# An attention and gated feed-forward kernel on one core: the copies that make high parts go from VectorE to ScalarE, the splits of x are spread out, and SyncE's transfers follow the program

## The chip, the core and the metric

The kernel runs on one core of a Trainium2 chip. The metric is device time in microseconds (us). The core has a matrix engine (TensorE, "PE" in the profile; its weight loads are "PEld"), VectorE ("DVE"), ScalarE ("ACT"), GpSimd ("POOL") and SyncE ("SP"). Here SP issues every transfer of the program and computes nothing. Each engine runs its own list of instructions in order; an instruction whose input is not ready holds up everything behind it on that engine.

## What is computed

```python
def _attn_ref(q, k, v, f):                      # q, k, v: (8, 8, 576, 64), f: (8, 8, 576)
    scores = matmul(q, k.T) / sqrt(64)
    cum = cumsum(log(clip(f, 1e-4, 1)))
    scores = where(causal, -1e9, scores + cum[:, None] - cum[None, :])
    attn = exp(scores - max(scores)); attn = attn / (sum(attn) + 1e-9)
    return matmul(attn, v)
def _moe_ref(x, w_in, w_out):                   # x: (4608, 512), from attention's output
    h = x @ w_in                                # (4608, 2048)
    g = h * erf(softplus(h))
    return g @ w_out                            # (4608, 512)
```

Everything is float32 at the interface; the weights arrive as 64-bit floats and are turned into 32-bit ones on the chip.

## The kernel before

**Attention** takes the 64 pairs of batch and head two at a time: 32 pairs p, each in two halves, so 64 steps t in a software pipeline of six stages (lines 648 to 698). In step t the program has: loads of q, k and the decay c for the pair after next and of v for the pair before (`load`, line 472; `load_values`, line 485), scores on PE, exps on ACT, the reduction on DVE, the normalization and the masks on POOL, transposes and values on PE, and the store of a finished pair to a scratch tensor `xt_d` in DRAM (line 611). q, k and c have three buffers each, v has two. Between these stand pieces of work that turn the first weights into pairs of parts (`weight_work`, line 332).

**The feed-forward part** wants near-float32 products from float32r matmuls. So every operand is kept as two parts: a high part, which is the value rounded to float32r by a copy, and a low part, which is the value minus the high part. Each product is then three matmuls. For x the work is a two-by-two block scheme with seven products instead of eight: seven combinations of four loaded blocks of x (`t[0]` to `t[3]`, and the sum `t[4]`) are split into parts, in seven slots `x_0` to `x_6`, and multiplied with seven combinations of w_in.

The work is cut into 12 visits v (six blocks of 768 tokens, once for each half of the 2048 columns) of four steps each; step n is step k = n mod 4 of visit n div 4. A step (`step`, line 241) goes through seven products i = 0 to 6. For each it has six matmuls `m<-x,wi` (`product`, line 131), then the work that takes the result out of PSUM (`consume`, line 155: ACT for i = 0 and 2, as tiles `sa` and `h`; DVE for the others, as `sb`, `sc` and `h`), then about five of the 36 matmuls `y<-wo,gh` and `y<-wo,gl` (`down`, line 192) of step n - 2. PSUM has two banks for m: a product can only begin when the earlier result in its bank was taken out.

In step n the gates of step n - 1 are made: four softplus and four erf on ACT (lines 175 and 178; each of the two functions needs a table load), and in `gate` (line 180), after product 1, for each of four tiles on DVE `e = e * h` (line 184) and the high part `gh` (line 188), and on POOL the low part `gl` (line 189).

In the last step of a visit (k = 3) x of the next visit is split (`split_x`, line 111): after products 0 to 4 one slot each, in the order `x_0`, `x_5`, `x_1`, `x_4`, `x_6`, and after products 0 and 1 of the next step `x_2` and `x_3`. The high parts are DVE's (line 121) but for `x_4` and `x_6`, which are ACT's (line 119); the low parts are POOL's but for `x_0` and `x_6`, which are DVE's (line 123). Two differences that use other slots' sources are DVE's: line 125 right behind `x_0`, and `last_sum` (line 129) behind product 3, ahead of the instruction that takes out product 4. It overwrites `t[1]`, which POOL reads for the low part of `x_1`. The loads of `t` for a visit stand at the start of step k = 2 of the visit before (`load_x`, line 96).

From step 2 to step 18 a filler list of 108 items (`FILL`, line 63) is worked off between the products: it loads a piece of the weights (`lraw`), then ACT takes a magnitude (line 356; often with a table load ahead of it and another behind it), DVE does four operations on the bits, and each finished 32-bit block is split by a copy (line 383, DVE) and a difference (line 384, POOL). A piece has one buffer for `lraw`: the next load is issued when `join` (line 371) has been done (line 373), and the next magnitude is the next item on the list. Some parts go to DRAM and are loaded again for the second half of the columns.

**What sets the order.** The kernel marks ACT, PE, DVE and POOL as ordered by the program's own order (`ORDERED`, line 20). SP is not in that set: its transfers are put in order by a scheduler, which may move a transfer ahead of others that the program has first.

Of the kernel before, what the change touches and what calls it, by code (L numbers as in the profile page):

```python
# [19 lines left out]
ORDERED = {mybir.EngineType.Activation, mybir.EngineType.PE, mybir.EngineType.DVE, mybir.EngineType.Pool}  # L20
# [52 lines left out]
class Moe:  # L73

    def __init__(self, tc, xt_d, part_d, out, xs):
# [6 lines left out]
        self.fill, self.reload = [], None  # L82
# [28 lines left out]
    def split_x(self, v, i):  # L111

        nc = self.nc
        t, r = self.t[v], XSLOT[i]
        src = t[{0: 0, 5: 0, 1: 1, 4: 4, 6: 2, 2: 1, 3: 3}[r]]
        x = self.x_tile(v, r)
        h, l = x[:, 0], x[:, 1]
        if i in (3, 4):
            nc.scalar.copy(out=h, in_=src)
        else:  # L120
            nc.vector.tensor_copy(out=h, in_=src)  # L121
        eng = nc.vector if i in (0, 4) else nc.gpsimd
        eng.tensor_tensor(out=l, in0=src, in1=h.bitcast(F32), op=ALU.subtract)  # L123
        if i == 0:
            nc.vector.tensor_tensor(out=t[0], in0=t[4], in1=t[0], op=ALU.subtract)

    def last_sum(self, v):
        t = self.t[v]
        self.nc.vector.tensor_tensor(out=t[1], in0=t[1], in1=t[0], op=ALU.subtract)
# [50 lines left out]
    def gate(self, n, q):  # L180

        nc = self.nc
        e, h = self.e.pop((n, q)), self.h.pop((n, q))
        nc.vector.tensor_mul(e, e, h)  # L184
# [3 lines left out]
        nc.vector.tensor_copy(out=gh, in_=e)  # L188
# [52 lines left out]
    def step(self, n):  # L241
# [13 lines left out]
        for i in range(7):  # L255
# [8 lines left out]
            if after and k == HU - 1 and i < 2:  # L264
                self.split_x(v + 1, i)
# [25 lines left out]
def attention_moe(ctx, tc, q2, k2, vp, f, w_in, w_out, out):  # L291
# [40 lines left out]
    def weight_work(pieces, buf):  # L332
# [42 lines left out]
        def parts(m, to, dst, src, cut=None):  # L375
# [7 lines left out]
            nc.vector.tensor_copy(out=vh, in_=src)  # L383
# [40 lines left out]
    def early_buf(kind, m, shape, dt=F32):  # L424
        slot = {"raw": m % 2, "top": 2 + m % 2, "tt": 4}[kind]
# [6 lines left out]
    load_weight, todo = weight_work([(a, i) for a in range(HU) for i in range(2)] + [(0, 2), (0, 3)], early_buf)  # L432
# [325 lines left out]
```

## Time and profile before

| | |
|---|---|
| time of the runs, us | 1264.35, 1259.42, 1255.23; median 1259.42 |
| the profiled execution, us | 1255.74, its span 1254.0 |
| mean granted clock of PE | 0.963 |
| attention, to the first product of step 0 | 0 to 331.57 |
| steps 0 and 1, beside the end of attention | 331.57 to 362.14 |
| steps 2 to 19, with the weights' pieces up to step 18 | 362.14 to 755.19 |
| steps 20 to 46 | 755.19 to 1216.65 |
| the last step, and the matmuls `y` of the last two | 1216.65 to 1254.0 |
| busy share of the span | PE 90%, DVE 72%, ACT 54%, POOL 54% |

A row of the profile's groups has the line, the engine, the operation and the tiles (written <- read, buffer numbers left out), the shapes and the count; then busy time in us and the mean ns of one; then the idle time of the engine just ahead of these instructions, and what ended most of it. A row of a timeline has the start in us, the duration, engine, line and tiles, and in brackets the idle time ahead of it with what ended it. A row of windows has a stretch of the span, its length, the busy us (and count) of PE, PEld, DVE, ACT and POOL in it, the granted clock of PE, the share of the transfer engines and GB/s.

### The profile page before, as it was taken

To read this page: it belongs to the slowest core of one execution; us is meant where nothing else is said; L and a number is where in the kernel's file an instruction comes from. 1 tells how busy PE (TensorE), PEld (TensorE's weight loads), DVE (VectorE), ACT (ScalarE), POOL (GpSimd) and SP (SyncE) were. 2 spreads that over 40 slices of the span, in tenths; PEclk is the share of its full clock that TensorE was granted. 3 is DMA by queue.
4 is the path that set the end of the run, shared out by engine and by line. 5 is a ranking of instruction groups with operands and counts; after the bars stand their busy time and mean duration, and the time that the engine had idled before them with its cause. 6 is when DMAs were issued, how large, how long until landed. Compare 5 with 4: busy or idle time off the path is not lost. (4 is left out here: it accounts for less than half of the span.)

```text
span 1254.0 us, 21300 instructions
## 1 busy us (share of the span) xinstructions
PE 1124.1 (90%) x7384; PEld 969.9 (77%) x7384; DVE 906.4 (72%) x1990; ACT 674.4 (54%) x1452; POOL 679.0 (54%) x808
## 2 busy tenths in 40 slices
PE   8988899999997687887786889989898989899898
PEld 7877788887885576776675778878787878788787
DVE  5886799998768568688767786656667666766565
ACT  4876688888653454465354654544344434445442
POOL 4785778888935327355445464444545353544422
PEclk8999999999998888998998899999999999999999
DMA  7666877876221231443322413443131312122032
GB/s 262 195 215 193 282 242 244 250 225 194 68 87 48 86 109 51 125 137 93 109 92 72 157 50 132 179 179 115 51 101 38 113 38 78 37 67 84 1 101 68
DMA packets 74908, 155.83 MB, mean 124 GB/s; under 512 B 7472, under 2 KB 27184, under 8 KB 73776
## 3 DMA queue, kind: packets, MB, share of 16 engines
q1 hardware_dynamic: 74800, 154.47, 38.0%
q8 instruction: 59, 0.97, 0.3%
q14 instruction: 49, 0.40, 0.1%
HBM read 114.44 MB, written 39.99 MB: 123 GB/s over the span
## 5 line engine op out<-in xcount | busy, mean ns | idle before, releaser
L147 PE MATMUL m<-x,wi 128*128 128x384 f32 x2016 | 429.2, 349 | 87.0 <-DVE sc L168 47.2
L147 PEld LDWEIGHTS m<-x,wi 128*128 128x128 f32 x2016 | 372.1, 194 | 133.7 <-DVE sc L168 60.2
L206 PE MATMUL y<-wo,gh 128*128 128x512 f32 x1152 | 385.5, 403 | 18.6 <-DVE wo L383 16.4
L189 POOL TENSOR_TENSOR gl<-e,gh 128x384 fp32r<-128x384 f32 x192 | 228.1, 1188 | 296.5 <-DVE gh L188 270.5
L206 PEld LDWEIGHTS y<-wo,gh 128*128 128x128 f32 x1152 | 220.4, 193 | 53.8 <-DVE wo L383 17.7
L206 PE MATMUL y<-wo,gl 128*128 128x512 f32 x576 | 231.7, 402 | 0.0
L557 POOL TENSOR_SCALAR pr<-pr,st 128x576 f32<-128x576 f32 (+4 forms) x320 | 167.9, 545 | 58.6 <-DVE st L553 30.2
L175 ACT ACTIVATE e<-h 128x384 f32<-128x384 f32 x192 | 93.6, 521 | 194.5 <-DVE h L171 194.1
L188 DVE CAST gh<-e 128x384 fp32r<-128x384 f32 x192 | 186.1, 969 | 6.6
L547 ACT ACTIVATE pr<-pr,st 128x576 f32<-128x576 f32 (+3 forms) x320 | 176.6, 557 | 8.0 <-DVE st L535 8.0
L535 DVE CUSTOM_DVE_ANT_0 pr<-s,c 128x576 f32<-128x576 f32 (+3 forms) x320 | 136.8, 487 | 36.5 <-PE s L519 25.8
L123 POOL TENSOR_TENSOR x<-t,x 128x768 fp32r<-128x768 f32 x55 | 105.0, 1916 | 92.4 <-DVE x L121 85.7
L206 PEld LDWEIGHTS y<-wo,gl 128*128 128x128 f32 x576 | 111.5, 194 | 17.9
L184 DVE TENSOR_TENSOR e<-e,h 128x384 f32<-128x384 f32 x192 | 106.2, 553 | 22.0 <-ACT e L178 21.9
L596 PE MATMUL o<-pt,v 128*64 128x128 f32 (+1 forms) x1920 | 106.0, 264 | 11.0 <-DMA v<-in_vp_dram 7.6
L596 PEld LDWEIGHTS o<-pt,v 128*64 128x64 f32 x1920 | 97.2, 140 | 21.1 <-DVE st L535 5.1
L515 PE MATMUL s<-k,q 64*128 64x320 f32 (+4 forms) x768 | 109.8, 411 | 2.1 <-DVE st L535 2.1
L578 ACT COPY pt<-t 128x512 f32<-128x512 f32 x128 | 73.9, 577 | 69.9 <-PE t L569 68.1
L569 PE MATMUL t<-ident,pr 128*128 128x128 f32 x800 | 105.1, 277 | 4.7 <-ACT pt L578 2.7
L569 PEld LDWEIGHTS t<-ident,pr 128*128 128x128 f32 x800 | 87.3, 140 | 17.6 <-issue 11.1
L171 DVE TENSOR_TENSOR h<-m,sb 128x384 f32<-128x384 f32 x96 | 53.0, 554 | 60.8 <-PE m L147 59.9
L515 PEld LDWEIGHTS s<-k,q 64*128 64x128 f32 x768 | 72.6, 189 | 30.5 <-issue 15.3
(96 smaller groups left out, 1147.4 us busy)
## 6 DMA issues: line engine op xcount, KB each, us to landing
v<-in_vp_dram SPq DMA_DIRECT2D x32, 576.0 KB, 6.5
c<-cum_d SPq DMA_DIRECT2D x62, 288.0 KB, 5.6
t<-xt_d SPq DMA_DIRECT2D x44, 384.0 KB, 3.3
q<-in_q_dram SPq DMA_DIRECT2D x32, 320.0 KB, 3.2
k<-in_k_dram SPq DMA_DIRECT2D x32, 288.0 KB, 4.3
xt_d<-xo SPq DMA_DIRECT2D x32, 288.0 KB, 5.7
part_d<-yo SPq DMA_DIRECT2D x36, 256.0 KB, 2.0
yo<-part_d SPq DMA_DIRECT2D x36, 256.0 KB, 2.9
```

What stands on the lines that cost most here:

```text
L123: eng.tensor_tensor(out=l, in0=src, in1=h.bitcast(F32), op=ALU.subtract)
L147: nc.tensor.matmul(out=ps, lhsT=w[:, wp, ws], rhs=x[:, xp, kd], start=first and kd == 0 and j == 0, stop=kd == 1 and j == 2 and i in (1, 2 ...
L184: nc.vector.tensor_mul(e, e, h)
L188: nc.vector.tensor_copy(out=gh, in_=e)
L189: nc.gpsimd.tensor_tensor(out=gl, in0=e, in1=gh.bitcast(F32), op=ALU.subtract)
L206: yield nc.tensor.matmul(out=y[tb], lhsT=g[:, cs], rhs=w[:, f, wp], start=first, stop=last)
L515: nc.tensor.matmul(out=s[j][:, at:at + k1 - k0], lhsT=q[h, PAD + START[i]:PAD + END[i]], rhs=k[h, k0:k1], start=i > 0, stop=i not in (0, 3))
L535: nc.vector.tensor_tensor_reduce(out=to[:, ::-1] if j else to, in0=score, in1=decay_, scale=-0.125, scalar=BIG, op0=ALU.add, op1=ALU.min, ...
L547: nc.scalar.activation(out=seg, in_=seg, func=AF.Exp, bias=st[:, 0, j, m:m + 1], scale=-1.0, accum_out=st[:, 1, j, m:m + 1])
L557: nc.gpsimd.tensor_scalar(out=seg, in0=seg, scalar1=st[:, 2, j, m:m + 1], scalar2=1.0, op0=ALU.mult, op1=ALU.mult)
L569: nc.tensor.transpose(out=b[:, n * P:(n + 1) * P], in_=probs[t][:, at:at + P], identity=ident)
L596: nc.tensor.matmul(out=o[h, to:to + width], lhsT=v[:, ch, h], rhs=pt[:, at[j]:at[j] + width], start=n == 0, stop=n == len(parts) - 1, skip ...
```

## The change

SP joins the ordered engines. `gate` is cut in two: the products `e * h` stay after product 1, and a new `halve` after product 2 makes `gh` by ACT and `gl` by POOL. All high parts of x are now ACT's, in every visit; the low parts of slots 0 and 5 are DVE's, the other five POOL's. In the last step of a visit the splits stand behind products 2 to 6 and ahead of the next step's first product. The high parts of the later weights' pieces (those of steps 2 to 18) are ACT's. During attention the splits of the first visit begin at step 44 of 64 with the loads, go on with one piece of work each at steps 46, 48, 50 and 52, and end with one slot each in steps 59 to 63; before, all of it stood in steps 56 to 63. The early weights' buffers move from slots 0 to 4 to slots 1 to 4 and 6. No instruction is added or dropped; five high parts of x per visit, four `gh` per step and the high parts of the later weights go from DVE to ACT.

```diff
-ORDERED = {mybir.EngineType.Activation, mybir.EngineType.PE, mybir.EngineType.DVE, mybir.EngineType.Pool}
+ORDERED = {mybir.EngineType.Activation, mybir.EngineType.PE, mybir.EngineType.DVE, mybir.EngineType.Pool,
+           mybir.EngineType.SP}
...
-    def split_x(self, v, i):
...
-        if i in (3, 4):
-            nc.scalar.copy(out=h, in_=src)
-        else:
-            nc.vector.tensor_copy(out=h, in_=src)
-        eng = nc.vector if i in (0, 4) else nc.gpsimd
-        eng.tensor_tensor(out=l, in0=src, in1=h.bitcast(F32), op=ALU.subtract)
-        if i == 0:
-            nc.vector.tensor_tensor(out=t[0], in0=t[4], in1=t[0], op=ALU.subtract)
...
+    def split_x(self, v, r):
+
+        t = self.t[v]
         x = self.x_tile(v, r)
+        self.src[r] = t[{0: 0, 5: 0, 1: 1, 4: 4, 6: 2, 2: 1, 3: 3}[r]]
+        self.nc.scalar.copy(out=x[:, 0], in_=self.src[r])
+
+    def rest_x(self, v, r):
+
+        x = self.x[v, r]
+        eng = self.nc.vector if r in (0, 5) else self.nc.gpsimd
+        eng.tensor_tensor(out=x[:, 1], in0=self.src[r], in1=x[:, 0].bitcast(F32), op=ALU.subtract)
+
+    def both_x(self, v, r):
+        self.split_x(v, r)
+        self.rest_x(v, r)
+
+    def late_sum(self, v, j):
         t = self.t[v]
-        self.nc.vector.tensor_tensor(out=t[1], in0=t[1], in1=t[0], op=ALU.subtract)
+        self.nc.vector.tensor_tensor(out=t[j], in0=t[4 if j == 0 else 1], in1=t[0], op=ALU.subtract)
...
     def gate(self, n, q):
+        self.nc.vector.tensor_mul(self.e[n, q], self.e[n, q], self.h.pop((n, q)))
+
+    def halve(self, n, q):
...
-        nc.vector.tensor_copy(out=gh, in_=e)
+        nc.scalar.copy(out=gh, in_=e)
         nc.gpsimd.tensor_tensor(out=gl, in0=e, in1=gh.bitcast(F32), op=ALU.subtract)
...
+        if up and v and k == 0:
+            self.both_x(v, 3)
         if gates:
             self.softplus(n - 1, 0)
...
-            if after and k == HU - 1 and i < 2:
-                self.split_x(v + 1, i)
...
-            if after and k == HU - 1 and 2 <= i < 5:
+            if after and k == HU - 1 and i == 2:
+                self.split_x(v + 1, 0)
+            if gates and i == 2:
+                for q in range(4):
+                    self.halve(n - 1, q)
+            if after and k == HU - 1:
                 if i == 3:
-                    self.last_sum(v + 1)
-                self.split_x(v + 1, i)
-            if up and v and k == 0 and i < 2:
-                self.split_x(v, 5 + i)
+                    self.rest_x(v + 1, 0)
+                    self.late_sum(v + 1, 0)
+                    self.both_x(v + 1, 1)
+                elif i == 4:
+                    self.both_x(v + 1, 5)
+                elif i == 5:
+                    self.late_sum(v + 1, 1)
+                    self.both_x(v + 1, 4)
+                elif i == 6:
+                    self.both_x(v + 1, 6)
+                    self.both_x(v + 1, 2)
...
-            nc.vector.tensor_copy(out=vh, in_=src)
+            cast(out=vh, in_=src)
...
-            if NH - 8 <= t < NH:
-                start_x(t - NH + 8)
+            if NH - 20 <= t < NH - 10 and t % 2 == 0:
+                start_x((t - NH + 20) // 2)
+            if NH - 5 <= t < NH:
+                start_x(t - NH + 10)
...
-                                        + [(a, i) for a in range(HU, NU) for i in range(4)], late_buf)
+                                        + [(a, i) for a in range(HU, NU) for i in range(4)], late_buf, nc.scalar.copy)
```

In the listings that follow, a row is one instruction in its engine's list: line, operation, tile written <- tiles read, size. The line numbers of the changed kernel are some 16 to 23 higher.

**SP, in the middle of attention.** `ta` and `tb` are the four blocks of x for the first visit, loaded from `xt_d`; `xt_d<-xo` is the store of a finished pair, which they read. Before:

```order
L476 DMA q_937<-in_q_dram 128x640
L477 DMA k_938<-in_k_dram 128x576
L482 DMA c_941<-cum_d 128x576 x2
L488 DMA v_944<-in_vp_dram 128x1152
L611 DMA xt_d<-xo_868 128x576
L443 DMA ta<-xt_d 128x384
L346 DMA raw_1678<-in_w_in_dram 128x2x512
L476 DMA q_1105<-in_q_dram 128x640
L477 DMA k_1106<-in_k_dram 128x576
L482 DMA c_1109<-cum_d 128x576 x2
L488 DMA v_1112<-in_vp_dram 128x1152
```

After, the same two pairs, and then the place where the loads of x now stand:

```order
L497 DMA q_937<-in_q_dram 128x640
L498 DMA k_938<-in_k_dram 128x576
L503 DMA c_941<-cum_d 128x576 x2
L509 DMA v_944<-in_vp_dram 128x1152
L632 DMA xt_d<-xo_868 128x576
L362 DMA raw_1021<-in_w_in_dram 128x2x512
L497 DMA q_1105<-in_q_dram 128x640
L498 DMA k_1106<-in_k_dram 128x576
L503 DMA c_1109<-cum_d 128x576 x2
L509 DMA v_1112<-in_vp_dram 128x1152
```

```order
L632 DMA xt_d<-xo_3658 128x576
L460 DMA ta<-xt_d 128x384 x4
L460 DMA tb<-xt_d 128x384 x4
L362 DMA raw_3898<-in_w_out_dram 128x1024
L497 DMA q_3900<-in_q_dram 128x640
```

Before, the scheduler had put each of the eight loads of x right behind a store to `xt_d`, ahead of the next pair's q, k, c and v, in the first third of attention; now all eight stand together at step 44.

**DVE, in the last step of a visit without weights' work** (`sc` takes out product 3, the tiles `h_3`, `h_1`, `h_2` products 4, 5 and 6). Before, from the last gate on:

```order
L184 TENSOR_TENSOR e_3_10904<-e_3_10904,h_3_10852 128x384
L188 CAST gh_3_10946<-e_3_10904 128x384
L121 CAST x_1_10964<-t_1_10747 128x768
L168 TENSOR_TENSOR sc_10979<-m_2_10972,sb_10925 128x384
L129 TENSOR_TENSOR t_1_10747<-t_1_10747,t_0_10746 128x768
L171 TENSOR_TENSOR h_3_10997<-m_3_10990,sc_10979 128x384
L123 TENSOR_TENSOR x_6_10999<-t_2_10748,x_6_10999 128x768
L171 TENSOR_TENSOR h_1_11013<-m_2_10972,sb_10925 128x384
L171 TENSOR_TENSOR h_2_11026<-m_3_10990,sb_10925 128x384
```

After:

```order
L183 TENSOR_TENSOR e_3_10904<-e_3_10904,h_3_10852 128x384
L170 TENSOR_TENSOR sc_10971<-m_2_10964,sb_10921 128x384
L123 TENSOR_TENSOR x_0_10941<-t_0_10746,x_0_10941 128x768
L131 TENSOR_TENSOR t_0_10746<-t_4_10750,t_0_10746 128x768
L173 TENSOR_TENSOR h_3_10990<-m_3_10983,sc_10971 128x384
L123 TENSOR_TENSOR x_5_10992<-t_0_10746,x_5_10992 128x768
L173 TENSOR_TENSOR h_1_11006<-m_2_10964,sb_10921 128x384
L131 TENSOR_TENSOR t_1_10747<-t_1_10747,t_0_10746 128x768
L173 TENSOR_TENSOR h_2_11023<-m_3_10983,sb_10921 128x384
```

The difference that overwrites `t_1` has moved from ahead of product 4's removal to ahead of product 6's; two differences of slot 0 have come in behind `sc`, and no copy is left.

**ACT, in the same step and into the next one** (`sa` takes out the next step's product 0). Before:

```order
L165 COPY h_0_10961<-m_0_10892 128x384
L270 ACT_TABLE_LOAD
L119 CAST x_4_10982<-t_4_10750 128x768
L119 CAST x_6_10999<-t_2_10748 128x768
L175 ACTIVATE e_0_11042<-h_0_10961 128x384
L175 ACTIVATE e_1_11044<-h_1_11013 128x384
L160 COPY sa_11054<-m_0_11046 128x384
```

After, from the last high part of the gates on:

```order
L192 CAST gh_3_10955<-e_3_10904 128x384
L117 CAST x_1_10975<-t_1_10747 128x768
L117 CAST x_5_10992<-t_0_10746 128x768
L117 CAST x_4_11009<-t_4_10750 128x768
L117 CAST x_6_11025<-t_2_10748 128x768
L117 CAST x_2_11028<-t_1_10747 128x768
L117 CAST x_3_11045<-t_3_10749 128x768
L177 ACTIVATE e_0_11048<-h_0_10938 128x384
L177 ACTIVATE e_1_11050<-h_1_11006 128x384
L162 COPY sa_11060<-m_0_11052 128x384
```

Between the table load and the next step's first softplus, where two copies stood, there are now eleven: `x_0`, the four `gh` and the six that the second list shows; `x_2` waits for DVE's difference that overwrites `t_1`.

More of the change, by code (lines that the diff above doesn't have):

```diff
@@ L81, in __init__ @@
         self.h, self.e, self.g, self.y, self.yo = {}, {}, {}, {}, {}
-        self.fill, self.reload = [], None
+        self.fill, self.reload, self.src = [], None, {}
     def place(self, pos):
@@ L180, in gate @@
     def gate(self, n, q):
+        self.nc.vector.tensor_mul(self.e[n, q], self.e[n, q], self.h.pop((n, q)))
+    def halve(self, n, q):
         nc = self.nc
-        e, h = self.e.pop((n, q)), self.h.pop((n, q))
-        nc.vector.tensor_mul(e, e, h)
+        e = self.e.pop((n, q))
         pos, at = (4 * n + q) % 12, (4 * n + q) % 8
@@ L330, in attention_moe, with weight_work @@
         wi_tile(0, k)
-    def weight_work(pieces, buf):
+    def weight_work(pieces, buf, cast):
         raws, tops, work = {}, {}, []
@@ L424, in early_buf @@
     def early_buf(kind, m, shape, dt=F32):
-        slot = {"raw": m % 2, "top": 2 + m % 2, "tt": 4}[kind]
+        slot = {"raw": (1, 2)[m % 2], "top": (3, 4)[m % 2], "tt": 6}[kind]
         return xs.tile(shape, dt, name=f"{kind}{m}", tag=f"xs{slot}")
@@ L430, in late_buf @@
         return moe.eb.tile(shape, dt, name=f"l{kind}{m}", tag=tag, bufs=bufs)
-    load_weight, todo = weight_work([(a, i) for a in range(HU) for i in range(2)] + [(0, 2), (0, 3)], early_buf)
+    load_weight, todo = weight_work([(a, i) for a in range(HU) for i in range(2)] + [(0, 2), (0, 3)], early_buf,
+                                    nc.vector.tensor_copy)
     def start_x(j):
@@ L445, in start_x @@
             moe.x_sum(0, j - 1)
-        else:
-            for i in {3: [0], 4: [1], 5: [2], 6: [3, 4], 7: [5, 6]}[j]:
-                if i == 3:
-                    moe.last_sum(0)
-                moe.split_x(0, i)
+        elif j == 3:
+            moe.both_x(0, 0)
+            moe.late_sum(0, 0)
+        elif j == 4:
+            moe.both_x(0, 5)
+        else:
+            moe.both_x(0, [1, 4, 6, 2, 3][j - 5])
+            if j == 5:
+                moe.late_sum(0, 1)
     moe_pools = ctx.enter_context(ExitStack())
```

5 lines of the change are left out of this document (removed).

## The prediction

> **What bounds the kernel now.** I first read the page's busy shares: PE is busy 90% of the span, so at most a tenth can come back, less the clock it loses. I then cut the span at the starts of products, to see where PE is not full. The columns are the length, the busy us (and count) of PE, PEld, DVE, ACT and POOL, the granted clock, the transfers' share and GB/s:
>
> ```profile
> 331.57:362.14 30.57, 27.88 (x242) 25.73 (x243) 16.60 (x35) 15.17 (x31) 16.91 (x23) 0.94 0.12 40
> 362.14:755.19 393.05, 317.08 (x1406) 271.90 (x1406) 296.18 (x439) 193.25 (x290) 191.92 (x148) 0.91 0.30 97
> 755.19:1216.65 461.46, 432.26 (x2108) 382.28 (x2107) 296.57 (x442) 205.95 (x342) 208.85 (x152) 1.00 0.27 88
> ...
> 823.41:839.23 15.82, 15.82 (x80) 14.10 (x79) 8.67 (x14) 7.18 (x12) 8.55 (x6) 1.00 0.66 254
> 839.23:855.23 16.00, 15.99 (x79) 14.09 (x78) 9.39 (x15) 8.51 (x15) 4.53 (x4) 1.00 0.40 150
> 855.23:870.99 15.76, 15.76 (x80) 14.21 (x79) 8.89 (x14) 7.18 (x12) 8.18 (x6) 1.00 0.45 150
> 870.99:891.62 20.63, 16.26 (x79) 14.01 (x78) 16.65 (x21) 8.75 (x14) 10.65 (x8) 1.00 0.09 20
> ...
> 75.00:131.01 56.01, 44.98 (x507) 37.44 (x505) 42.23 (x162) 38.86 (x122) 38.50 (x77) 0.96 0.66 206
> 150.00:240.00 90.00, 90.00 (x1056) 74.83 (x1055) 82.62 (x313) 74.41 (x232) 74.13 (x144) 1.00 0.77 243
> ```
>
> The four rows in the middle are one visit without weights' work. Three of its steps are full of PE work at 15.8 to 16.0 us, so PE bounds them and nothing can be won there. The fourth, in which x is split, takes 20.63 us with PE idle for 4.37. With a fourth step of 15.8 us a visit would take 63.4. The 18 steps with weights (2 to 19) take 393.05 us against 18/4 x 63.4 = 285.3: an excess of 107.7. PE idles 76.0 us there, so each idle us costs 107.7 / 76.0 = 1.42: the granted clock is 0.91. The last two rows are attention: 1056 matmuls in 90 us when it runs full, 507 in 56 us between 75 and 131 us.
>
> Who is waited for, in the weights' steps (PE's and DVE's waits from 362 to 800 us) and then in attention (PE's and SP's):
>
> ```profile
> PE m L147 <- DVE sc L168: 34.5, 13, 5.5
> PE y L206 <- DVE wo L383: 16.4, 3, 6.8
> PE m L147 <- ACT sa L160: 12.1, 5, 2.8
> PE m L147 <- DVE h L171: 9.4, 7, 2.1
> ...
> DVE ltop L359 <- ACT ltop L356: 39.7, 9, 5.4
> ...
> PE o L596 <- DMA v<-in_vp_dram: 7.6, 3, 3.2
> ...
> SPq L443 <- DMA xt_d<-xo: 62.3, 8, 8.9
> ```
>
> Most is DVE, late in taking results out of PSUM. The timeline of the split step shows how:
>
> ```profile
> 883.24 0.54 DVE L168 TENSOR_TENSOR sc<-m,sb 128x384 f32<-128x384 f32 x1
> 883.84 1.32 PE L147 MATMUL m<-x,wi 128*128 128x384 f32 x6 [1.61 <-DVE sc L168]
> 884.14 3.61 POOL L123 TENSOR_TENSOR x<-t,x 128x768 fp32r<-128x768 f32 x2
> 886.02 2.54 DVE L129 TENSOR_TENSOR t<-t,t 128x768 f32<-128x768 f32 x1 [2.23 <-POOL x L123]
> 888.48 0.55 DVE L171 TENSOR_TENSOR h<-m,sc 128x384 f32<-128x384 f32 x1
> 889.08 1.31 PE L147 MATMUL m<-x,wi 128*128 128x384 f32 x6 [2.76 <-DVE h L171]
> ```
>
> `sc` stands behind four gates with their copies, 1.61 us late. Then DVE waits 2.23 us for POOL to have read t[1], works 2.54, and only then takes out product 4: 2.76 us more for PE.
>
> **Prices.** The kinds of work that move, and their nearest rows:
>
> ```profile
> L188 DVE CAST gh<-e 128x384 fp32r<-128x384 f32 x192 | 186.1, 969 | 6.6
> L119 ACT CAST x<-t 128x768 fp32r<-128x768 f32 x22 | 18.3, 836 | 20.2 <-PE m L147 18.4 <-POOL gl L189 1.9
> L165 ACT COPY h<-m 128x384 f32<-128x384 f32 x48 | 22.9, 478 | 15.2 <-PE m L147 13.8
> L175 ACT ACTIVATE e<-h 128x384 f32<-128x384 f32 x192 | 93.6, 521 | 194.5 <-DVE h L171 194.1
> L225 ACT COPY yo<-y 128x512 f32<-128x512 f32 x18 | 10.4, 578 | 29.4 <-PE y L206 22.0 <-issue 7.4
> L123 POOL TENSOR_TENSOR x<-t,x 128x768 fp32r<-128x768 f32 x55 | 105.0, 1916 | 92.4 <-DVE x L121 85.7
> L189 POOL TENSOR_TENSOR gl<-e,gh 128x384 fp32r<-128x384 f32 x192 | 228.1, 1188 | 296.5 <-DVE gh L188 270.5
> L125 DVE TENSOR_TENSOR t<-t,t 128x768 f32<-128x768 f32 x11 | 10.5, 958 | 1.2
> L129 DVE TENSOR_TENSOR t<-t,t 128x768 f32<-128x768 f32 x11 | 28.1, 2550 | 23.4 <-POOL x L123 23.4
> L356 ACT ACT_TABLE_LOAD x15 | 19.2, 1283 | 69.5 <-DMA lraw<-in_w_out_dram 34.9 <-DMA lraw<-in_w_in_dram 29.3 <-issue 5.3
> L356 ACT ACTIVATE ltop<-lraw 128x512 f32<-128x512 f32 x22 | 14.7, 667 | 35.4 <-DMA lraw<-in_w_in_dram 26.0 <-DMA lraw<-in_w_out_dram 7.3 <-DMA t<-xt_d 1.9
> ```
>
> A high part of a gate costs DVE 0.97 us; on ACT I take 0.48, as its 384-wide copy (bounds 0.42, half the 768-wide cast, and 0.58, the 512-wide copy). A 256-wide one is 0.36 by the slope between 478 and 836 ns. So each step loses 3.9 us of DVE work and gains 1.9 of ACT. In the steps that are full of PE work that wins nothing.
>
> **SP in attention: 12 us won.** Eight times SP sat on a store to `xt_d` before it could issue a load of x, 62.3 us in all, with the next pair's q, k, c and v queued behind; v then came late. At 1056 matmuls in 90 us, 507 take 43.2 us, not 56.0: 12.8 lost, of which the late v named 7.6 and what followed the rest. At step 44 the stores that these loads read are long done. They cost eight issues and 1.5 MB at about 240 GB/s, some 6 us of transfers, which the lead of two pairs hides; uncovered, up to 6 us. I take 12, with 6 and 13 as the ends. At the start, q and k of the second pair now come behind the store of `cum`:
>
> ```profile
> 9.72 0.47 SPq L642 DMA_DIRECT2D cum_d<-cum  x1
> 14.77 1.76 SPq L482 DMA_DIRECT2D c<-cum_d  x4
> ```
>
> Between these two SP has 4.6 us to wait in any case, room for both issues: nothing; uncovered, 1 us. At the end of attention POOL has five low parts where it had five and two sums, so I add 1 us there, with 0 and 3 as ends.
>
> **The split step without weights: 15 us won.** I walk through it by durations, from its first product at 870.99; a product comes every 15.8 / 7 = 2.26 us.
>
> ```profile
> 865.54 1.02 POOL L189 TENSOR_TENSOR gl<-e,gh 128x384 fp32r<-128x384 f32 x1 [0.39 <-DVE gh L188]
> ...
> 877.17 1.28 ACT L270 ACT_TABLE_LOAD   x1
> ```
>
> ACT is through its table load at 7.4, as now, copies x_0 until 8.3, the gates until 10.3 and x_1 until 11.1. POOL starts `gl` at 8.9, needs 1.0 to 1.2 for each of the four, and 1.9 for the low part of x_1: done between 14.8 and 17.2, as DVE's three differences in between (`x_0`, t[0], `x_5`) do or don't hold it up. The one that overwrites t[1] follows, 0.96 us alone or 2.55 behind POOL's next one: 16 to 20. Behind it are two waiters. DVE takes out product 6, which the next step's second product needs at 18.0. ACT copies x_2 and x_3, makes two softplus (0.5 each) and copies `sa`: 3.2 us more, so 19.2 to 23.2, where the next step's third product needs it at 20.3. PE then waits 0 to 3.0 us; I take 2.0, as POOL is the more likely to be held up, in place of 4.37. Over six such steps that is 6 x 2.4 = 14, and 1 for DVE's relief in the others: 15, with 8 and 29 (all of PE's idle time from 755 us on) as ends. In the other steps `gl` is done by 7.4 + 0.5 + 4 x 1.2 = 12.7, before the next softplus overwrites the tile it reads: no wait comes in there.
>
> [...]
>
> **The steps with weights: 50 us won.** What stays: a piece's load starts when `join` is done and the magnitude is the next item.
>
> ```profile
> 645.08 0.33 SPq L346 DMA_DIRECT2D lraw<-in_w_out_dram  x1
> ...
> 649.50 1.28 ACT L356 ACT_TABLE_LOAD   x1 [11.35 <-DMA lraw<-in_w_out_dram]
> ...
> 654.12 1.32 PE L147 MATMUL m<-x,wi 128*128 128x384 f32 x6 [2.14 <-ACT sa L160]
> ```
>
> Landing takes 4.4 us, then two table loads and two softplus stand ahead of `sa`. SP issues `lraw` at once already, so its order wins nothing here. DVE's 39.7 us of waiting for magnitudes stays too. I count PE's idle time after the change: these waits for `sa`, 12.1 us as now, plus 3 for a few more; 4.5 split steps at 2.0, that is 9; the waits for wo in steps 3 to 5, 16.4 now, 8, as DVE, rid of 3.9 us of copies, reaches `join` 2 to 3 us sooner; and 9 for ACT's new load, 2 a visit. ACT gets 72 gates x 0.48 = 35, 22 casts of x x 0.84 = 18 and some 42 weights' blocks of 0.36 to 0.58, 18: 71 us on 193.25, or 14.7 us a step against PE's 15.8, full enough to be late now and then. The sum is 41 us idle, x 1.42 = 58: 107.7 - 58 = 50 won. The ends are 24 and 75, from the cases below.
>
> [...]
>
> **Sum.** The profiled execution took 1255.74, its span 1254.0. 12 + 1 + 15 + 50 = 78: 1178. Its time lies 3.7 below the median of the runs shown; taking half of that I predict **1180 us**.
>
> **Rivals.** (a) *Only transfers' waits are left*: ACT's copies hide wholly, the split steps are full. Idle in the weights' steps: 15 and 8 us, x 1.42 = 33, so 75 won; 29 in the later steps, 13 in attention: 117, or 1139 us. For it: ACT sat idle over half the time there. Against: x_2 and `sa` queue behind POOL, as worked out. (b) *ACT becomes the bound with weights*: 14.7 us a step and its waits for `lraw`, 69.5 + 35.4 = 105 us over 18 steps, 5.8, make 20.5, or 369 us in all: 24 won. With 4 in the split steps and 13 in attention: 1215 us. For it: the two add up where a transfer lands late. Against: part of that waiting is slack. (c) *Slower*: every copy on ACT lies on the chain from softplus over `gh` and `gl` to the next product, and DVE's relief buys nothing. Then all 71 us come on top and only attention's 12 come off: 1315 us. It decides once more than 12 of the 71 lie on that path with no relief elsewhere. For it: ACT's list is in order, and `sa` stands behind all of them. Against: `sa` is waited for 12.1 us now, DVE 60. (d) *The SP order doesn't mend attention*, v being late for want of bandwidth: 1192 us. Against: 243 GB/s flow where PE is full, 206 where it waits.
>
> **Chances.** The forecast 0.61, (a) 0.16, (b) 0.13, (c) 0.05, (d) 0.05. The range 1141 to 1222 us leaves out (c) and half of (a) with a little of (b): two in ten. The forecast's own range is 1160 to 1205. About 1% is what a measurement can tell from no change here: faster by more 0.92, within 1% 0.03, slower 0.05.
>
> **What would show it.** Right: between 75 and 131 us PE is full and no wait for v is left; `gh` takes ACT about 0.48 us; a split step without weights takes 17 to 19 us, its wait now on `sa` or the last `h`; the weights' steps take about 343 us, with waits for `sc` nearly gone and those for `sa` the largest. Wrong: a split step over 20 us, ACT over 0.9 busy with PE waiting for it throughout the weights' steps, or gates' differences on POOL so late that `y` waits for `gl`.

## The result and the profile after

The changed kernel took **1213.01 us** (median of four runs, 1212.26 to 1216.35); the kernel before, run beside it, 1259.42 (1255.23 to 1264.35; a fourth, disturbed run of 1292.91 is left out here and in the ratio). The ratio is 0.9635, with a 95% interval of 0.9586 to 0.9683: 3.65% faster. The forecast was 1180, its range 1141 to 1222. So the sign and the range held, but of the 78 us forecast 43.5 came by the profiled executions (1255.74 - 1212.26), 46.4 by the medians. The profiled execution took 1212.26 us, its span 1210.5. I cut it into the same stages as before (the columns are those of the windows in the prediction: length, busy us and count of PE, PEld, DVE, ACT and POOL, clock, transfers' share, GB/s), with the weak stretch of attention last:

```profile
350.74:731.09 380.35, 315.15 (x1405) 272.36 (x1405) 210.11 (x299) 255.99 (x425) 182.33 (x144) 0.91 0.29 99
731.09:1172.02 440.93, 429.16 (x2107) 383.42 (x2107) 193.38 (x305) 273.49 (x484) 207.86 (x156) 1.00 0.27 94
...
75.00:131.01 56.01, 56.01 (x664) 46.65 (x662) 51.40 (x199) 45.95 (x145) 46.79 (x91) 1.00 0.77 243
```

| stage | before, us | after, us | change | forecast |
|---|---|---|---|---|
| attention | 331.6 | 320.2 | -11.4 | -12 + 1 |
| steps 0 and 1 | 30.6 | 30.5 | 0 | 0 |
| steps 2 to 19, with weights | 393.1 | 380.4 | **-12.7** | **-50** |
| steps 20 to 46, without | 461.5 | 440.9 | -20.5 | -15 |
| end | 37.4 | 38.5 | +1.1 | 0 |

Attention came out as worked out, and the stretch from 75 to 131 us is now full: 664 matmuls where there were 507. The steps without weights won somewhat more than forecast. The error lies in the weights' steps. PE idled 76.0 us there and still idles 380.35 - 315.15 = 65.2. PE's, ACT's and DVE's waits of that stage, from 350 to 745 us, show who holds it up now (the window runs 14 us past the stage, and one wait for `h` of 2.8 us lies there, in step 20):

```profile
PE m L149 <- ACT sa L162: 25.6, 10, 5.7
PE m L149 <- DVE h L173: 19.5, 10, 4.1
PE y L210 <- ACT wo L399: 18.9, 3, 10.3
...
ACT lhi L399 <- DVE ltop L387: 30.5, 8, 7.0
ACT wo L399 <- DVE ltop L387: 23.0, 6, 5.7
...
ACT lhi L399 <- DMA wi_d<-lhi: 11.2, 6, 3.6
...
ACT lhi L399 <- POOL llo L400: 9.5, 5, 3.3
...
PE y L210 <- POOL wo L400: 2.4, 4, 0.9
```

The wait for `sc`, 34.5 us before, is gone; the one for `sa` has doubled from 12.1, and the one for `wo` has grown from 16.4, now named after ACT. The four rows of ACT are new as a kind: ACT's casts of weights wait for DVE's `join`, for the stores of finished parts and for POOL's low parts, 74 us in all. ACT was busy 255.99 of 380.35 us there, 67%: it is not full, it is held up. The operations cost what was forecast, by the groups of the steps without weights:

```profile
L192 ACT CAST gh<-e 128x384 fp32r<-128x384 f32 x104 | 45.6, 510 | 0.2
L117 ACT CAST x<-t 128x768 fp32r<-128x768 f32 x42 | 33.3, 832 | 36.5 <-DVE t L131 36.4
L183 DVE TENSOR_TENSOR e<-e,h 128x384 f32<-128x384 f32 x104 | 51.1, 553 | 20.8 <-ACT e L180 20.7
```

`gh` is 45.6 / 104 = 0.44 us of ACT's time apiece (0.48 taken), a high part of x 33.3 / 42 = 0.79 (0.84 taken).

A split step without weights (977.49 to the next step at 993.24) and the wait that follows it, from the timeline:

```profile
992.01 9.79 POOL L123 TENSOR_TENSOR x<-t,x 128x768 fp32r<-128x768 f32 x5
993.90 2.58 DVE L131 TENSOR_TENSOR t<-t,t 128x768 f32<-128x768 f32 x1 [2.25 <-POOL x L123]
...
997.10 1.28 PE L149 MATMUL m<-x,wi 128*128 128x384 f32 x6 [1.49 <-DVE h L173]
```

The walk forecast the difference that overwrites `t[1]` to end 16 to 20 us after the step's first product; it ended at 996.48, 19.0 after. PE's wait is 1.49 us (2.0 taken) and falls into the next step, so the four steps of a visit now take 17.98, 15.75, 15.75 and 15.75 us on average, where they took 15.90, 16.44, 15.75 and 20.80. The signs named beforehand came out for `v`, for `gh`, for `sc` and `sa` and, with the wait counted where it falls, for the split step; the weights' steps, at 380 us in place of about 343, did not.

### The profile page after: what moved, and what is told of

It is laid out like the page before. It is cut to its first block, busy times and chain, and to the rows that moved or that the text cites. A ratio compares the mean times of both kernels' runs of the same rounds, so it can differ in the third digit from the quotient of the medians.

```text
span 1210.5 us, 21366 instructions
## 1 busy us (share of the span) xinstructions
PE 1115.7 (92%) x7384; PEld 968.0 (80%) x7384; DVE 708.3 (59%) x1696; ACT 813.2 (67%) x1746; POOL 666.6 (55%) x808
## 5 line engine op out<-in xcount | busy, mean ns | idle before, releaser
L193 POOL TENSOR_TENSOR gl<-e,gh 128x384 fp32r<-128x384 f32 x192 | 213.3, 1142 | 393.2 <-ACT gh L192 368.4
L210 PE MATMUL y<-wo,gh 128*128 128x512 f32 x1152 | 384.0, 401 | 21.4 <-ACT wo L399 18.9
L578 POOL TENSOR_SCALAR pr<-pr,st 128x576 f32<-128x576 f32 (+4 forms) x320 | 165.1, 538 | 49.6 <-DVE st L574 29.6
L183 DVE TENSOR_TENSOR e<-e,h 128x384 f32<-128x384 f32 x192 | 95.4, 559 | 56.3 <-ACT e L180 56.1
L210 PEld LDWEIGHTS y<-wo,gl 128*128 128x128 f32 x576 | 111.2, 193 | 17.6
L165 DVE TENSOR_TENSOR sb<-m,sa 128x384 f32<-128x384 f32 x48 | 26.7, 557 | 143.8 <-PE m L149 88.5
L123 POOL TENSOR_TENSOR x<-t,x 128x768 fp32r<-128x768 f32 x55 | 108.5, 2003 | 4.1 <-ACT x L117 4.1
L117 ACT CAST x<-t 128x768 fp32r<-128x768 f32 x77 | 61.3, 832 | 53.6 <-DVE t L131 53.4
```

What stands on the lines that cost most here:

```text
L123: eng.tensor_tensor(out=x[:, 1], in0=self.src[r], in1=x[:, 0].bitcast(F32), op=ALU.subtract)
L183: self.nc.vector.tensor_mul(self.e[n, q], self.e[n, q], self.h.pop((n, q)))
L193: nc.gpsimd.tensor_tensor(out=gl, in0=e, in1=gh.bitcast(F32), op=ALU.subtract)
L210: yield nc.tensor.matmul(out=y[tb], lhsT=g[:, cs], rhs=w[:, f, wp], start=first, stop=last)
L578: nc.gpsimd.tensor_scalar(out=seg, in0=seg, scalar1=st[:, 2, j, m:m + 1], scalar2=1.0, op0=ALU.mult, op1=ALU.mult)
```

## The experiments

"After" is the changed kernel; none of the eleven others leaves out a part of the work. The lengths of the stages come from each run's own profiled execution, and PE's idle time in the last two is the stage's length less PE's busy time:

| run | time, us | ratio to before, 95% | attention | steps 2 to 19 | steps 20 to 46 | PE idle in the two |
|---|---|---|---|---|---|---|
| before | 1259.42 | | 331.6 | 393.1 | 461.5 | 76.0 / 29.2 |
| after | 1213.01 | 0.9635 (0.9586 to 0.9683) | 320.2 | 380.4 | 440.9 | 65.2 / 11.8 |
| e1 | 1193.37 | 0.9519 (0.9484 to 0.9553) | 321.7 | 365.3 | 438.1 | 54.5 / 10.5 |
| e2 | 1221.40 | 0.9740 (0.9698 to 0.9782) | 331.5 | 384.1 | 440.0 | 68.5 / 11.0 |
| e3 | 1209.05 | 0.9643 (0.9605 to 0.9681) | 320.6 | 378.9 | 436.0 | 66.9 / 8.9 |
| e4 | 1244.15 | 0.9917 (0.9888 to 0.9946) | 318.0 | 389.7 | 468.4 | 70.0 / 30.2 |
| e5 | 1184.53 | 0.9407 (0.9369 to 0.9444) | 318.2 | 360.8 | 435.4 | 49.5 / 8.2 |
| e6 | 1169.32 | 0.9281 (0.9237 to 0.9324) | 319.9 | 353.5 | 425.3 | 51.9 / 0.0 |
| e7 | 1157.96 | 0.9201 (0.9166 to 0.9236) | 317.3 | 334.0 | 435.3 | 34.3 / 8.2 |
| e8 | 1214.40 | 0.9643 (0.9595 to 0.9690) | 318.8 | 383.4 | 437.8 | 66.6 / 8.8 |
| e9 | 1139.79 | 0.9068 (0.9038 to 0.9098) | 317.1 | 326.7 | 425.3 | 30.8 / 0.0 |
| e10 | 1189.22 | 0.9464 (0.9425 to 0.9502) | 321.7 | 357.8 | 438.4 | 52.5 / 9.2 |
| e11 | 1204.69 | 0.9594 (0.9514 to 0.9675) | 322.4 | 365.7 | 447.0 | 55.8 / 16.2 |

The kernel before took 1255.83, 1255.95, 1259.29 and 1256.07 us beside e1 to e4, e5 to e8, e9 and e10, and e11, so a few us between runs of different groups say little; there the stages are the better witness. And stages move by 2 to 7 us where nothing was changed in them.

### e1: the later weights' high parts back on DVE

```diff
-    ... late_buf, nc.scalar.copy)
+    ... late_buf, nc.vector.tensor_copy)
```

> The changed kernel with one part undone: the high parts of the later weights' pieces are VectorE's again. Theory (ACT is held up, not full: its copies of the weights stand in its list behind DVE's bit operations, POOL's differences and the stores of finished parts, with the copy sa behind them): PE's waits for ACT's sa fall from 25.6 us to about 12 and those for wo from 18.9 to about 10 in the steps with weights, whose stage takes 345 to 360 us in place of 380; in all 1180 to 1195 us. Rival (ACT is full, 14.7 us a step and its waits for transfers): ACT is rid of 18 us of work spread over 18 steps, 1 us a step, so at most 18 us go and more likely 5: 1195 to 1210 us, with sa still the largest wait. Rival (DVE was the bound and is so again): 1213 us or more, waits for sc come back.

1193.37 us, 19.6 less than after by the medians and 14.6 by the ratios (0.0116 of 1255.83). The weights' steps fell by 15.1 us to 365.3. The stage's window and PE's waits in e1, 350 to 745 us:

```profile
350.64:715.91 365.27, 310.77 (x1405) 269.84 (x1405) 233.05 (x341) 240.49 (x383) 185.28 (x145) 0.92 0.32 104
```

```profile
PE m L149 <- DVE h L173: 20.6, 12, 4.0
PE y L210 <- DVE wo L399: 15.5, 2, 10.4
PE m L149 <- ACT sa L162: 12.0, 5, 3.0
```

Only 42 casts moved, some 16 us of ACT's work (255.99 to 240.49), and the wait for `sa` went from 25.6 back to 12.0, its value before the change. The rest of what was expected fell short: the wait for `wo` is 15.5, not about 10, and the stage is above the 345 to 360 us named. How the casts hold `sa` up stands in ACT's timeline of after, in step 7 (463.7 on), with PE's row behind it:

```profile
463.49 0.41 ACT L399 CAST lhi<-ltt 128x256 fp32r<-128x256 f32 x1 [3.27 <-POOL llo L400]
465.74 0.41 ACT L399 CAST lhi<-ltt 128x256 fp32r<-128x256 f32 x1 [1.84 <-DMA wi_d<-lhi]
466.71 0.41 ACT L399 CAST lhi<-ltt 128x256 fp32r<-128x256 f32 x1 [0.57 <-POOL llo L400]
468.94 0.40 ACT L399 CAST lhi<-ltt 128x256 fp32r<-128x256 f32 x1 [1.82 <-DMA wi_d<-lhi]
```

```profile
473.97 1.33 PE L149 MATMUL m<-x,wi 128*128 128x384 f32 x3 [5.65 <-ACT sa L162]
```

Four casts of 0.41 us take ACT from 460.2 to 469.3, because each waits for something else: 7.5 us of the 9.1 are waits. The table load, the magnitude, the softplus and `sa` stand behind them in the list, and PE stands still for 5.65 us.

### e2 and e4: SP's order taken away, and given to the kernel before alone

```diff
-ORDERED = {mybir.EngineType.Activation, mybir.EngineType.PE, mybir.EngineType.DVE, mybir.EngineType.Pool,
-           mybir.EngineType.SP}
+ORDERED = {mybir.EngineType.Activation, mybir.EngineType.PE, mybir.EngineType.DVE, mybir.EngineType.Pool}
```

e4 is the reverse edit, on the kernel before.

> The changed kernel with one part undone: SP's transfers are put in order by the scheduler again. Theory (program order on SP is worth only what it gives attention, since the loads of x no longer stand ahead of q, k, c and v): if the scheduler again moves the loads of x up behind the stores, attention takes 331 us in place of 320 and the time is 1222 to 1227 us; the later stages stay within 3 us. Rival (moving the program's loads of x to step 44 was enough, the order does nothing): 1213 us. Rival (SP's order matters in the feed-forward part too): the stage from step 2 to 19 changes by over 5 us.

> The kernel before, with SP's transfers in the program's order and nothing else changed. Theory: attention runs full, 320 us in place of 331.6, the rest as before: 1244 to 1249 us on the scale on which the profiled execution of the kernel before is 1255.7. Rival (the scheduler's order also had a use later, where loads were moved ahead): attention wins the same 11 us and the steps with weights lose 5 us or more: 1250 us or over. Rival (the loads of x, all at step 56 in the program, come too late for sums and splits there): the end of attention loses 3 us or more.

e2 took 1221.40 us, 8.4 more than after, and most of what it lost lies in attention: 331.5 us, as before the change (the weights' steps read 3.7 longer). e4 took 1244.15, 11.7 us less than the kernel before beside it, with attention at 318.0. PE's and SP's waits in attention, of e2 and then PE's of e4:

```profile
PE o L616 <- DMA v<-in_vp_dram: 8.1, 3, 4.1
...
SPq L459 <- DMA xt_d<-xo: 61.5, 8, 8.9
```

```profile
PE t L570 <- POOL pr L558: 2.8, 3, 1.4
```

With the scheduler's order the eight loads of x sit behind stores again and v comes late again; with the program's order neither wait is there, in either kernel. So the 12 us of attention belong to SP's order alone. Outside attention it is worth nothing that these runs can show (e4's later steps even read 7 us longer than those of before).

### e3: the late difference written over another tile

```diff
-        self.nc.vector.tensor_tensor(out=t[j], in0=t[4 if j == 0 else 1], in1=t[0], op=ALU.subtract)
+        self.nc.vector.tensor_tensor(out=t[0], in0=t[4 if j == 0 else 1], in1=t[0], op=ALU.subtract)
...
-        self.src[r] = t[{0: 0, 5: 0, 1: 1, 4: 4, 6: 2, 2: 1, 3: 3}[r]]
+        self.src[r] = t[{0: 0, 5: 0, 1: 1, 4: 4, 6: 2, 2: 0, 3: 3}[r]]
```

What still reads the tile then is slot 5, whose high part is ACT's and whose low part is DVE's own and stands ahead in the same list; so the difference need not wait for POOL.

> The changed kernel, but DVE's second difference of a split is written over t[0], which only ACT and DVE read, in place of t[1], which POOL reads; x_2 is split from t[0]. The same numbers are computed. [...] Rival (ACT's queue, x_2, x_3 and sa, decides, not DVE): a wait for sa of 1 to 1.5 us takes the place of the wait for h, 1210 to 1213 us.

1209.05 us: 4 less than after by the medians, no different by the ratios; the steps without weights are 4.9 us shorter. For the case that DVE's wait of 2.25 us for POOL is the cause of PE's 1.49, 1185 to 1200 us had been forecast; that was not reached, and no wait for `sa`, which the rival expects, has come in. The timeline of a split step in e3, and PE's waits from 745 to 1200 us:

```profile
1115.65 1.30 DVE L131 TENSOR_TENSOR t<-t,t 128x768 f32<-128x768 f32 x1
1116.10 10.13 POOL L123 TENSOR_TENSOR x<-t,x 128x768 fp32r<-128x768 f32 x5
...
1122.59 6.64 DVE L183 TENSOR_TENSOR e<-e,h 128x384 f32<-128x384 f32 x4 [1.21 <-ACT e L180]
```

```profile
PE m L149 <- DVE sc L170: 7.2, 6, 1.2
```

The wait for POOL is gone, and the difference takes 1.30 us in place of 2.58. But of six waits of 1.49 us six of 1.20 are left, now on `sc`: while POOL runs its five low parts back to back, DVE's four gates take 6.64 us, or 1.66 each, against the mean of 0.553 in after's group shown above. So the wait on the tile is gone as intended, but most of what was to be won with it is not: beside POOL's row DVE is now late by its gates in place of the difference.

### e5 and e6: both edits; then a shorter row of POOL's

```diff
-        eng = self.nc.vector if r in (0, 5) else self.nc.gpsimd
+        eng = self.nc.vector if r in (0, 5, 6, 2) else self.nc.gpsimd
```

e5 is e1 and e3 together; e6 is e5 with this line.

> The changed kernel with the later weights' high parts on VectorE and DVE's second difference written over t[0]: the two edits tried singly before (1193.4 and 1209.05 us beside 1213). Theory (two separate waits): the gains add, 19.6 + 4 = 24 us: 1187 to 1191 us. Rival (with DVE earlier, POOL's row of five low parts lies on DVE's gates instead, so the second edit is worth nothing once DVE also has the weights' copies): 1192 to 1196 us.

> The kernel of the two edits, and the low parts of slots 6 and 2 are VectorE's too (POOL keeps 1, 4 and 3). [...]

e5 took 1184.53 us: the two gains add up (weights' steps 360.8, later ones 435.4), and the time is 2.5 us below the range of the theory. e6 took 1169.32, another 15 us and 7 below the 1176 to 1185 forecast for it: with three low parts on POOL and four on DVE, every step from 20 on takes 15.75 us, PE's idle time there is 0.0 us, and the weights' steps are 353.5. DVE has more work than in e5 and is less late, so in the split step it was POOL's long row, not DVE's load, that made DVE late.

### e7: two buffers for the raw weights

On e5:

```diff
-        tag, bufs = {"raw": ("raw", 1), ...
+        tag, bufs = {"raw": ("raw", 2), ...
...
-            load(m + 1)
+            load(m + ahead)
...
     load_weight(0)
+    load_weight(1)
```

with `ahead` = 2 for the later weights.

> The kernel of the two edits, and the later weights' pieces are loaded two ahead into two buffers. Theory (what is left in the steps with weights is the transfer between join and the next magnitude, 4 us on ACT's and DVE's lists): PE's waits for sa (12 us) go, those for wo (15.5) fall under 6, and the clock rises with them: the stage takes 325 to 340 us in place of 365, 1155 to 1172 us in all. [...]

1157.96 us, 26.6 less than e5: the largest gain of one edit here. The weights' steps take 334.0. PE's waits from 350 to 745 us, the one for `sa` in e5 and then those in e7:

```profile
PE m L149 <- ACT sa L162: 8.4, 5, 2.7
```

```profile
PE y L210 <- DVE wo L399: 11.8, 3, 7.3
PE m L149 <- DVE sb L165: 7.7, 3, 4.1
PE m L149 <- DVE h L173: 7.5, 5, 2.5
PE m L149 <- DVE sc L170: 6.4, 3, 3.2
...
PE m L149 <- ACT sa L162: 0.2, 1, 0.2
```

With the next piece already loaded when ACT reaches its magnitude, `sa` is waited for 0.2 us. So the waits for `sa` that the forecast kept were the landing of `lraw`, as it said. For `wo` 11.8 us remain, of 15.4 in e5; under 6 had been expected. Part of what makes it late shows in after, at step 4, where PE waits longest (all engines, in order of time), with two rows of the same step in before behind it:

```profile
396.14 1.28 ACT L372 ACT_TABLE_LOAD   x1 [2.96 <-DMA lraw<-in_w_out_dram]
...
398.89 5.96 POOL L123 TENSOR_TENSOR x<-t,x 128x768 fp32r<-128x768 f32 x3 [3.89 <-ACT x L117]
399.20 1.78 DVE L380 TENSOR_SCALAR lraw<-ltop 128x512 int32<-128x512 int32 x1
401.02 2.17 DVE L382 SCALAR_TENSOR_TENSOR lraw<-lraw 128x512 int32<-128x512 int32 x1
403.22 2.17 DVE L387 SCALAR_TENSOR_TENSOR ltop<-ltop,lraw 128x512 int32<-128x512 int32 x1
...
406.10 0.80 PE L210 MATMUL y<-wo,gh 128*128 128x512 f32 x1 [10.31 <-ACT wo L399]
```

```profile
414.94 0.69 DVE L371 SCALAR_TENSOR_TENSOR ltop<-ltop,lraw 128x512 int32<-128x512 int32 x1
...
416.15 0.79 PE L206 MATMUL y<-wo,gh 128*128 128x512 f32 x1 [6.78 <-DVE wo L383]
```

The piece's transfer lands late; then the last three operations of `join` take 1.78 + 2.17 + 2.17 = 6.12 us beside POOL's three low parts. Over all pieces of after they are (count, then least, median and longest in ns):

```profile
L380 DVE TENSOR_SCALAR lraw<-ltop x22: 411/429/1960, 360.2 to 712.0; 128x512 int32<-128x512 int32 x22
L382 DVE SCALAR_TENSOR_TENSOR lraw<-lraw x22: 692/693/2210, 360.7 to 713.6; 128x512 int32<-128x512 int32 x22
L387 DVE SCALAR_TENSOR_TENSOR ltop<-ltop,lraw x22: 679/693/2328, 361.8 to 714.7; 128x512 int32<-128x512 int32 x22
```

By the medians they would take 1.82 us, 4.3 less. In before, where POOL has no low part of x at this place, they take 0.42 + 0.69 + 0.69 = 1.80 us, and PE waits 6.78. In e6, where two of the three low parts are DVE's, they take 1.80 us again:

```profile
402.12 0.69 DVE L387 SCALAR_TENSOR_TENSOR ltop<-ltop,lraw 128x512 int32<-128x512 int32 x1
```

So the 4.3 us are POOL's doing. But e6 has those two low parts, 2.82 us, on DVE's list ahead of the three operations, and PE's wait only falls from 10.50 in e5 to 9.16.

### e8 and e10: the high parts of the gates back on DVE

```diff
-        nc.scalar.copy(out=gh, in_=e)
+        nc.vector.tensor_copy(out=gh, in_=e)
```

e8 is after with this line, e10 is e1 with it.

> The changed kernel with one part undone: the gates' high parts gh are VectorE's again, at the changed place behind product 2. Theory (DVE's 3.9 us a step of copies made it late): waits for sc come back in the last steps of visits and in the steps with weights, DVE is over 0.8 busy there: 1222 to 1240 us. Rival (ACT's list is what is long in the steps with weights, and gh is the largest part of what it got, 35 us): the stage from step 2 to 19 gets shorter by 5 us or more, and the later one longer by up to 15: 1210 to 1222 us.

> The changed kernel with both other moves to ACT undone: the later weights' high parts and the gates' gh are VectorE's again; SP's order, x's high parts on ACT and the spread of x stay. Theory (of the change, SP's order and the spread of x earned everything; gh on ACT nothing, the weights' copies on ACT cost 20 us): 1189 to 1197 us, as without the weights' move alone (1193.4). Rival (gh on ACT is worth something once the weights' copies are off ACT's list, and was hidden by them): 1200 to 1215 us, with waits for sc and h longer in the steps with weights.

e8 took 1214.40 us against after's 1213.01, with ratios of 0.9643 and 0.9635; e10 took 1189.22 against e1's 1193.37. Moving 192 copies between the engines is worth nothing, or 4 us the wrong way, and the intervals of e10 and e1 overlap. e8's time lies in the range of its rival, but neither stage moved as that rival had it: the weights' steps are 3 us longer and the later ones 3 shorter. PE's waits in e8, 350 to 745 us, beside those of after:

```profile
PE m L149 <- ACT sa L162: 26.1, 12, 5.5
PE y L210 <- ACT wo L399: 18.4, 3, 10.4
PE m L149 <- DVE h L173: 13.9, 9, 3.1
PE m L149 <- DVE sc L170: 6.7, 6, 1.7
```

DVE has four copies a step back (3.9 us by the row of before), and the waits for `wo` (18.4 against 18.9) and `sa` (26.1 against 25.6) stand where they were. What `gh` decides is only whether PE waits for `h` or for `sc`: 20.6 us together here, 19.5 in after.

### e11: the places and SP's order, no copy moved

On e10, the high parts of x also back on DVE, but for two a visit as before the change:

```diff
-        self.nc.scalar.copy(out=x[:, 0], in_=self.src[r])
+        copy = self.nc.scalar.copy if r in (4, 6) else self.nc.vector.tensor_copy
+        copy(out=x[:, 0], in_=self.src[r])
```

> The changed kernel with every move to ACT undone: x's high parts but those of slots 4 and 6 are VectorE's again too, in the changed places. What stays is SP's order and the places of the splits. Theory (the places earned it, not the engine): 1189 to 1200 us, beside 1189.22 with x's high parts on ACT; the steps from 20 on take 435 to 445 us. Rival (x's high parts had to leave DVE, where five copies of 0.6 to 1.0 us that wait for PE and for DVE's own differences stand ahead of h): the last and the first steps of a visit lose 2 us or more each, the stage from 20 on takes 452 us or more, 1210 us in all.

1204.69 us (1203.6 to 1205.8). That is above the range named for the theory by 5 us and does not meet the rival either; it lies between them, as do its 447.0 us from step 20 on. No copy has changed engines here against before, and it is still 8 us faster than the whole change by the medians (the intervals of the two ratios overlap). Moving x's high parts to ACT is worth 1204.69 - 1189.22 = 15.5 us more. PE's waits of e11, 345 to 1150 us:

```profile
PE m L150 <- DVE h L174: 23.6, 19, 2.9
...
PE m L150 <- DVE sc L171: 12.3, 9, 2.4
```

e10 has 14.9 and 9.6 us in their place. The copies lengthen DVE's list exactly in the split step: the last step of a visit takes 17.02 us on average in e11 and 15.75 in e10 and after. But e11 holds more than the places of x's splits: the copies and low parts of the gates stand behind product 2, the low part of slot 6 has gone to POOL and that of slot 5 to DVE, and x's first splits are spread over attention. None of these was tried alone.

### e9: everything that helped the weights' and the split steps

e6 and e7 together; `gh` stays on ACT.

> The changed kernel with all four edits of the runs before: the later weights' high parts on VectorE, the second difference over t[0], the low parts of slots 6 and 2 on VectorE, and the weights' pieces loaded two ahead. Theory (transfers' waits and POOL's long row are two separate causes): to 1158 us comes off what POOL's shorter row won before, 10 us in the steps from 20 on and some in the first steps of visits with weights: 1141 to 1150 us, with no idle time of PE from step 20 to 46. Rival (with the transfers hidden, DVE is the long list in the steps with weights, and two more low parts on it cost what they win): 1150 to 1158 us.

**1139.79 us**, 0.9068 of before, the fastest of all, and 1 us below the range of the theory. The stages of steps 2 to 19 and 20 to 46 in e9:

```profile
347.54:674.26 326.72, 295.91 (x1406) 259.91 (x1406) 250.85 (x351) 242.16 (x384) 177.35 (x137) 0.97 0.35 116
674.26:1099.60 425.34, 425.34 (x2108) 383.39 (x2107) 220.65 (x318) 273.20 (x484) 191.31 (x141) 1.00 0.28 97
```

The later stage is PE's work and nothing else. Of the 30.8 us that PE still idles with weights, 10.9 are the waits for `wo` in steps 3 to 5.

## Why the prediction was right and wrong

The runs make a ladder from before to after:

| part | from, us | to, us | worth |
|---|---|---|---|
| SP in the program's order | 1255.83 (before) | 1244.15 (e4) | -11.7 |
| x's and the gates' parts in their new places, two low parts swapped | 1244.15 (e4) | 1204.69 (e11) | -39.5 |
| x's high parts to ACT | 1204.69 (e11) | 1189.22 (e10) | -15.5 |
| `gh` to ACT | 1189.22 (e10) | 1193.37 (e1) | +4.2 |
| later weights' high parts to ACT | 1193.37 (e1) | 1213.01 (after) | **+19.6** |

Its rungs are medians of runs of different groups, so the 4.2 of `gh` is no more than what the kernel before moves between them (1255.83 to 1259.29); by the ratios the last rung is 14.6.

**SP in attention** (12 forecast): right, 11.7, by the mechanism named. Rival (d), v late for want of bandwidth, falls: the stretch moves 243 GB/s when full, against 206.

**The split step without weights** (15 forecast): the mechanism is right to the tile, as the timeline above shows (its end at 19.0 us lies in the 16 to 20 of the walk), and so is the size. By the mean steps, the six split steps won 6 x (20.80 - 15.75) = 30.3 and the seven first steps of a visit, into which the wait has moved, gave 7 x (17.98 - 15.90) = 14.6 back: 15.7 where 14 was forecast. Of the 14.6 the first of them, step 20, which follows the last split with weights, gave 4.6: it takes 20.39 us. The rest of the 20.5 is in the second steps, 7 x (16.44 - 15.75) = 4.8, for which the forecast had 1: the visit that it went by has 16.00 there, most later ones 16.6. The late difference took 2.58 us, as the one beside POOL's low parts had before (2.55), and PE's wait is 1.49 us, in the middle of the 0 to 3.0 of the walk. In e3, where that difference does not wait for POOL and takes 1.30 us, DVE's gates are slow beside POOL's row (1.66 us each) and cost PE nearly as much (1.20 us).

**The weights' steps** (50 forecast, 12.7 found): here a step failed. The prediction counted 41 us of PE's idle time; 65.2 are there, and the factor was nearly right: (380.35 - 285.3) / 65.2 = 1.46 against 1.42. Set against the count, term by term:

- *`sa` 15 "and 9 for ACT's new load"*: 24, and `sa` is waited for 25.6. The size is right, and the weights' casts on ACT are the cause (e1: idle from 65.2 to 54.5, `sa` to 12.0). But the price is no load, as the prediction took it. ACT's 14.2 us a step (255.99 / 18) are under the 14.7 forecast, and a third of ACT's time is free; the casts bring their own waits into ACT's list, ahead of `sa`. Seen so, the prediction could have said that this part alone loses what it lost, some 15 us of the stage, and that the change was better without it.
- *Waits for `wo`, "8, as DVE, rid of 3.9 us of copies, reaches `join` 2 to 3 us sooner"*: 18.9, and 2.4 more for its low part on POOL; 13 too few. **This is the step that failed.** `join` does not stand behind copies: e8 gives DVE those of the gates back, and the wait stays at 18.4. It stands behind a transfer into a single buffer and, in the new places, works beside POOL's low parts: in step 4 PE waited 6.78 us before, and waits 9.92 in e11, whose copies are all where they were before. The second buffer takes the sum from 15.4 (e5) to 11.8 (e7), the shorter row from 15.4 to 14.0 (e6); with both (e9) 10.9 are left, and what makes those was not tried.
- *Split steps, 4.5 x 2.0 = 9*: the waits for `h`, by which they show, are 16.7 within the stage; 8 too few. The walk by which 2.0 was found holds in steps without weights; with them, `h` is up to 4.1 us late: 11.7 us lie in the four steps behind a split (4, 8, 12, 16), near 3 each, and 5.1 elsewhere. Counted within the stage over `h`, `sb` and `sc`, after has 17.6, e1 21.4, e7 20.4 and e9, with POOL's shorter row as well, 17.9; so neither ACT's casts nor the transfer is the cause. What makes these late was not tried.

**The relief of DVE**, by which the prediction explained much of the gain in the weights' steps, is shown wrong for `gh`, the largest block of copies, and right for x's high parts, which stand in the split step's own list (15.5 us, about half of it from step 20 on: 447.0 to 438.4). Most of the gain, 39.5 us, comes from where the parts stand: between e4 and e11 the weights' steps lose 24.0 us and the later ones 21.4 (14.5 against the stage of before, as e4's reads long), and attention takes 4.4 more.

**The rivals.** (b) gave 1215 us, 2 from the result, by another road: ACT is 67% busy in that stage, not full. It had 4 us won in the split steps and 24 with weights, and 20.5 and 12.7 were found, so the near hit is two errors that cancel. (c), ACT's list as the way to a slower kernel, had the mechanism of the weights' casts, at 19.6 us where it took 71 for all copies. (a) fell: PE still waits for far more than transfers.

**The clock.** After's granted clock is 0.91 in the weights' steps, with waits up to 10.3 us. It was below 1 with a shorter wait too: step 20 of after has one wait, of 2.82 us, and a granted clock of 0.92, which 1.4 us behind the wait is 0.50 for a while:

```profile
739.00:741.00 2.00, 2.00 (x8) 1.90 (x7) 0.18 (x1) 1.97 (x4) 2.00 (x2) 0.50 0.00 0
```

Before has the same once in its later stage (0.95 in step 35, whose longest wait is 2.76 us; step 31, with one as long, has 1.00); the mean of 1.00 hides it. And at a granted 1.00 an idle us still costs more than itself: the six other first steps of a visit take 17.58 us, so (17.58 - 15.75) / 1.49 = 1.23. Which part of the 1.46 with weights is the clock's stays open.

## What to carry to other kernels

A copy moved to a half-idle engine brings its waits along: before pricing the work, list what each moved instruction must wait for, and who stands behind it in the new engine's order; here some 16 us of casts cost 15 to 20 us of time on an engine that was a third free. Where an engine is late, ask which of its instructions is long in that very place and beside whose work, rather than how much it has to do in all: a shorter row on POOL and a second load buffer gave 15 and 27 us, while taking 192 copies off DVE gave nothing. And a loss that is named after one engine (`wo` after DVE) has to be followed to the transfer and the neighbour behind it before it is halved in a forecast.

## What the runs showed of the hardware

Beside a long row on POOL, DVE's instructions took longer, and not only the one difference that the prediction reckoned with (0.96 to 2.55 us in before): the 128x384 gates took 1.66 us each in e3 against a mean of 0.553 in after, and the 128x512 integer operations of `join`, the first of which reads one tile only, took 1.78 and 2.17 in step 4 of after against medians of 0.43 and 0.69. POOL ran on at 10.13 / 5 = 2.03 us a low part in e3 meanwhile, against the 1.92 of its mean in before, so DVE bore nearly all of the loss. The granted clock of PE was 0.50 for a while behind a wait of 2.82 us (step 20 of after).
